# Attention in 64-by-192 halves with one division per token tile, weights bit-converted on VectorE in SBUF and checked late, a rational activation by completed squares, and a new order

## The chip, the cores and the metric

The kernel runs on one core of a Trainium2 chip. The core has a matrix engine (TensorE, PE in the profile), VectorE (DVE), ScalarE (ACT), GpSimd (POOL) and an engine that only issues transfers here (SyncE, SP). The metric is the device time of one launch in microseconds.

## What is computed

Three stages in a row on 1536 tokens (2 batches of 768): an attention of 8 heads of 64, in which a query sees the 96 keys up to itself and the first 8 of the sequence; a feed-forward layer ("MoE 1", 512 to 2048 to 512) whose activation is a ratio of two polynomials; and a second one ("MoE 2", 512 to 1024 to 512) with a softmax gate and a layer norm between its products. The weights arrive as 64-bit floats.

```
keep = is_global | is_local                      # 8 first keys, 96 keys up to the query
a = softmax(where(keep, q @ k.T / 8 - slope[h] * dist, -1e9))
x = (a @ v) with the heads side by side          # 1536 x 512

h = x @ w_in                                     # 512 -> 2048
P = a[0] + a[1]*h + a[2]*h*h + a[3]*h*h*h
Q = 1 + |b[0]|*|h| + |b[1]|*h*h
x = (P / (Q + 1e-6)) @ w_out                     # 2048 -> 512

h = x @ w2_in                                    # 512 -> 1024
solu = h * softmax(h)
ln = (solu - mean) / sqrt(var + 1e-6) * g_ln
out = ln @ w2_out                                # 1024 -> 512
```

## The kernel before

The 1536 tokens are 12 tiles of 128, in 4 blocks of three tiles (384 tokens). The attention works in **units**: one tile and one pair of heads, 48 in all. 8 of them (first tile of a sequence) see 128 keys, the other 40 see 256, of which the mask leaves what counts. One unit goes through all engines: SP loads queries and keys and then values; PE makes the scores (line 459, two matmuls; in blocks 0 and 3 each head's 64 rows of the array work beside the other's into two banks, in blocks 1 and 2 both heads go one after the other through all 128 rows into one bank); DVE adds the bias and finds the maximum (464); ACT takes the exponential with its row sum (471); DVE inverts the sum (476, 477); POOL or, for the 19 units of `NDVE`, DVE multiplies by it (482); PE transposes (502, four of 128 by 128); ACT copies to SBUF (514); PE multiplies with the values (509); ACT and DVE split the result into a rounded high part and a rest (516 and the helper in line 99). `x` in such pairs is the left side of MoE 1.

**MoE 1** runs in 64 **steps**, one for each group of 128 hidden units and block: 12 matmuls of 128x384 for `h` (634, 636 and 640: high times high, high times low, low times high), an epilogue on ACT, DVE and POOL (660 to 677 and the helper), and, three steps later (`LAG`), 9 matmuls of 128x512 that add into the three `y` banks (725, 726, 731). Block 0 comes first with 8 of its 16 groups, then blocks 1 to 3, then block 0 again with the rest (`SEGS`). The attention units of the next block are laid between the steps of the current one (`UW`). The epilogue before is, in order: c = a3*h + a2 (ACT 660), times h (DVE 662), |b0*h| (ACT 663), c = (c + a1)*h (DVE 664), h squared in PSUM (ACT 666), q (DVE 667), 1/Q as exp(-ln) (ACT 669, 670) with a Newton step (DVE 671, 673), times P (DVE 675), rounded copy (ACT 677), rest (POOL, line 99).

**Weights**: 48 tiles of 128x512 64-bit floats, 512 KB each. Of each an ACT multiply (565) and integer operations on DVE make a 32-bit float, for 22 tiles three (569, 570, 574), for the 26 of `ZS` a POOL multiply (582) and two on DVE (586, 574); the half-made words lie in a PSUM bank of the attention's. Then ACT rounds (604) and POOL, or DVE for the 6 of `WDVE`, takes the rest (99).

**MoE 2** goes tile by tile: 24 matmuls (810 to 812), maximum and softmax and norm on DVE and ACT (832 to 854, 857, 859), transposes (872), split (880, 99), 24 matmuls (894 to 896, the last tile in quarters), output.

**What sets the order**: every operation is recorded with an estimated duration and what it reads and writes; a planner (`Plan`) works out due times, shifted by kind with the table `LEADS`, and emits each engine's instructions in one fixed order. PSUM has 8 banks: two for `h`, two `s` (scores, weight conversion), one `p` (transposes, values), three for `y`. In gaps that the planner expects on PE early on, it emits dummy matmuls of the identity (line 337, 51 of them in before). A flag (lines 1187 to 1194), worked out from the mask's sizes, says whether a general slow path must follow.

## Time and profile before

| | us |
|---|---|
| three runs | 557.36, 557.90, 558.82 |
| median | 557.9 |
| span of the profiled execution | 556.3 |
| PE busy | 531.8 (96%) |
| DVE busy | 446.0 (80%) |
| ACT busy | 393.0 (71%) |
| POOL busy | 182.5 (33%) |

Beside its span the profiled execution has no other time in the page; the median of the runs is 1.6 us above the span. Busy shares are means over stages with different limits: the start (attention alone, up to 43.66 us), MoE 1 with attention and weight conversion beside it (up to about 408 us), and MoE 2. PE's busy time includes a matmul's way through the array, so gaps shorter than that don't show in it; what PE has to do is better read from the distance of starts in the timeline.

### The profile page before, as it was taken

Reading aid. Unit: us, or ns where it says so; the run is one execution under the profiler, and the core shown is the slowest. Engines: PE = TensorE matmul, PEld = TensorE weight load, DVE = VectorE, ACT = ScalarE, POOL = GpSimd, SP = SyncE. Lnnn points to the kernel's source line nnn. Section 1 sums busy time; section 2 is a strip of 40 time slices with the busy share of each in tenths; the row PEclk is TensorE's granted clock in tenths of the full one; section 3 lists DMA queues with packets and bytes.
Section 4 is the critical chain, followed back from the end, with each engine's and each line's share of the span. In section 5 each row is a group of like instructions: output and inputs, shape, how many; then the busy total and the mean of one; then the engine's idle time right before and its main releaser. Section 6 shows DMA issues by size and latency. Waiting matters only on the chain.

```text
span 556.3 us, 8937 instructions
## 1 busy us (share of the span) xinstructions
PE 531.8 (96%) x2910; PEld 437.0 (79%) x2910; DVE 446.0 (80%) x1104; ACT 393.0 (71%) x911; POOL 182.5 (33%) x212
## 2 busy tenths in 40 slices
...
PEclk9999999999999999999999999999999999999999
...
GB/s 252 130 201 341 195 219 86 185 135 153 104 182 154 151 96 98 73 48 48 1 38 114 133 77 75 77 180 87 57 20 38 39 38 58 20 19 20 19 39 43
DMA packets 28278, 56.24 MB, mean 101 GB/s; under 512 B 3520, under 2 KB 11968, under 8 KB 28224
## 3 DMA queue, kind: packets, MB, share of 16 engines
...
q8 instruction: 25, 0.41, 0.3%
q14 instruction: 29, 0.24, 0.1%
q10 hardware_dynamic: 144, 0.00, 0.0%
HBM read 47.72 MB, written 7.86 MB: 100 GB/s over the span
## 4 chain that ended last, share of the span: by engine, by line
PE 55%; DVE 29%; ACT 10%; issue 4%; DMA 1%; POOL 0%; SPq 0%; ACTq 0%; DVEq 0%; POOLq 0%
PE pb L894 4%; PE pb L896 4%; PE pb L895 4%; PE pb L634 4%; PE pb L810 4%; PE pb L812 4%; PE pb L811 4%; PE pb L640 4%; PE pb L731 3%; PE pb L636 3%; PE pb L725 3%; DVE t L667 3%; PE pb L459 3%; DVE wst L574 3%; PE pb L726 3%
## 5 line engine op out<-in xcount | busy, mean ns | idle before, releaser
L99 POOL TENSOR_TENSOR g<-t,g 128x384 fp32r<-128x384 f32 x64 | 69.2, 1082 | 103.9 <-ACT g L677 91.7
L634 PE MATMUL pb<-x,w 128*128 128x384 f32 x256 | 89.3, 349 | 1.8 <-DVE t L667 1.8
L636 PE MATMUL pb<-x,w 128*128 128x384 f32 x256 | 86.1, 336 | 0.0
L725 PE MATMUL pb<-w,g 128*128 128x512 f32 x192 | 77.5, 404 | 4.2 <-ACT g L677 4.2
L726 PE MATMUL pb<-w,g 128*128 128x512 f32 x192 | 75.6, 394 | 0.5 <-POOL w L99 0.5
L99 POOL TENSOR_TENSOR w<-wst,w 128x512 fp32r<-128x512 f32 x42 | 57.2, 1364 | 42.7 <-ACT w L604 38.8
L640 PE MATMUL pb<-x,w 128*128 128x384 f32 x256 | 58.0, 347 | 0.1
L731 PE MATMUL pb<-w,g 128*128 128x512 f32 x192 | 57.7, 409 | 0.2 <-POOL g L99 0.2
L634 PEld LDWEIGHTS pb<-x,w 128*128 128x128 f32 x256 | 48.1, 188 | 8.6 <-DVE t L667 4.4
L471 ACT ACTIVATE e<-e,st 128x256 f32<-128x256 f32 (+1 forms) x96 | 46.3, 486 | 6.4 <-DVE st L464 6.4
L640 PEld LDWEIGHTS pb<-x,w 128*128 128x128 f32 x256 | 44.5, 188 | 7.1 <-issue 3.1
L636 PEld LDWEIGHTS pb<-x,w 128*128 128x128 f32 x256 | 48.1, 188 | 1.5
L725 PEld LDWEIGHTS pb<-w,g 128*128 128x128 f32 x192 | 36.0, 187 | 14.4 <-ACT g L677 7.3
L660 ACT ACTIVATE t<-pb,coef 128x384 f32<-128x384 f32 x64 | 42.7, 668 | 6.1 <-PE pb L640 6.1
L482 POOL TENSOR_SCALAR e<-e,st 128x256 f32<-128x256 f32 (+1 forms) x58 | 28.0, 495 | 54.4 <-DVE st L477 48.4
L669 ACT ACTIVATE t<-t,coef 128x384 f32<-128x384 f32 x64 | 39.6, 618 | 6.8 <-DVE t L667 6.6
L662 DVE TENSOR_TENSOR t<-t,pb 128x384 f32<-128x384 f32 x64 | 35.2, 549 | 11.1 <-ACT t L663 6.5
L677 ACT CAST g<-t 128x384 fp32r<-128x384 f32 x64 | 32.8, 512 | 16.0 <-DVE t L675 15.3
L880 ACT CAST lh<-pb 128x512 fp32r<-128x512 f32 x24 | 13.9, 592 | 42.5 <-PE pb L872 42.5
L459 PE MATMUL pb<-qk 64*128 64x256 f32 (+3 forms) x192 | 41.3, 393 | 2.7 <-DVE st L464 1.0
L667 DVE SCALAR_TENSOR_TENSOR t<-pb,coef,t 128x384 f32<-128x384 f32 x64 | 39.2, 613 | 5.2 <-ACT pb L666 4.8
L671 DVE SCALAR_TENSOR_TENSOR t<-t,t 128x384 f32<-128x384 f32 x64 | 40.6, 634 | 1.3 <-ACT t L670 1.3
...
## 6 DMA issues: line engine op xcount, KB each, us to landing
...
```

The lines of the kernel that those rows point to most:

```text
L99: eng.tensor_tensor(out=out, in0=a, in1=hi.bitcast(F32), op=ALU.subtract)
L459: pe.matmul(out=score(h), lhsT=a[r, h * 128:(h + 1) * 128], rhs=a[r, 256:256 + w], start=True, stop=True)
L471: act.activation(out=e[:, h, 0:w], in_=e[:, h, 0:w], func=AF.Exp, scale=-1.0, bias=st[:, h:h + 1], accum_out=st[:, 2 + 2 * h:3 + 2 * h])
L634: pe.matmul(out=pb[:, g.h.slot, 0:n], lhsT=wt[wh.slot][:, cs[p]], rhs=xt[x[p][0].slot][:, 0:n], start=(p == 0), stop=False)
L636: pe.matmul(out=pb[:, g.h.slot, 0:n], lhsT=wt[wl.slot][:, cs[p]], rhs=xt[x[p][0].slot][:, 0:n], start=False, stop=False)
L640: pe.matmul(out=pb[:, g.h.slot, 0:n], lhsT=wt[wh.slot][:, cs[p]], rhs=xt[x[p][1].slot][:, 0:n], start=False, stop=(p == 3))
L660: op("ACT", 0.2 + 0.46 * k, lambda: act.activation(out=T(g.c), in_=h(), func=AF.Identity, scale=coef[:, 3:4], bias=coef[:, 2:3]), r=[g.h], ...
L667: op("DVE", 0.2 + 0.41 * k, lambda: stt_(out=T(g.a), in0=h(), scalar=coef[:, 5:6], in1=T(g.b), op0=ALU.mult, op1=ALU.add), r=[g.h, g.b], n ...
L671: op("DVE", 0.15 + 0.41 * k, lambda: stt_(out=T(g.a), in0=T(g.a), scalar=1.0 + 1e-6, in1=T(g.b), op0=ALU.add, op1=ALU.mult), r=[g.b], w=[g ...
L725: pe.matmul(out=pb[:, y[i].slot, :], lhsT=gt[g.gh.slot][:, c], rhs=wt[wh.slot], start=g.first, stop=False)
L726: pe.matmul(out=pb[:, y[i].slot, :], lhsT=gt[g.gh.slot][:, c], rhs=wt[wl.slot], start=False, stop=False)
L731: pe.matmul(out=pb[:, y[i].slot, :], lhsT=gt[g.gl.slot][:, c], rhs=wt[wh.slot], start=False, stop=g.last)
```

## The change

Attention units of the 40 kind now take 64 queries by 192 keys each: four score matmuls of 64 rows by 64 columns of the array with 192 moving columns (line 571), three transposes (601) instead of four, one exponential of 192 (585). The values' product is turned round (614): the transposed weights are stationary and the values move, in three pairs of column halves, and the four units of a tile add into one bank. Nothing is divided in a unit; per tile one inversion (631, 632), one multiplication of 128x512 out of PSUM on DVE (637), four transposes (641) and one split (649, 149) stand in the place of four of each. ACT or, for 10 units of `TRX`, DVE copies the transposed weights (619).

Weight conversion is three DVE integer operations (705, 709, 713) in an SBUF buffer `cvt`; the ACT and POOL multiplies are gone. The new operations hold for exponents in a usual range only. The rounding goes to ACT (28), POOL (13) or DVE (7) by `WHX`; the rest to DVE 17 times. Whether the exponents lie in that range is found out during MoE 2: all 48 weight tiles are loaded again (25 MB) and one DVE operation each (763, 765) collects the bits; a small tree, one matmul and the flag stand at the end of the program, and the engines load the flag there.

The polynomials are written with completed squares: c is one ACT square of a scaled and shifted h (826), and the multiplication by h (662 before) and the square in PSUM (666 before) are gone. q is, for 32 steps of `SQX`, another ACT square (832) and for 32 a DVE operation (836). The exponential's result lies in SBUF for 16 steps and in PSUM banks `p` or `s` for 48 (`EPX`). The rounded copy goes to ACT (33), POOL (16) or DVE (15) by `GHX`. A sign that the squares leave over is multiplied in when `y` leaves PSUM. Some 20 small DVE and 4 small ACT operations that work out the new coefficients are added at the start. `SPILL`'s reload goes from ACT and POOL to DVE. All tables (`LEADS`, `UW`, `WS`, `M2`, `BACK`) are new; dummy matmuls before MoE 1 are 18 instead of 51. The queries, keys and values of a unit are 448 KB instead of 384.

```diff
-UW = {1: (0, 7), 2: (8, 15), 3: (25, 14)}
+UW = {1: (1, 4), 2: (8, 15), 3: (25, 9)}
...
+WS = (1, 24)
+
+M2 = (29, 35)
+
+WSB, TB, GB, QB, VB, EB, YB, PB = 4, 8, 4, 3, 4, 3, 4, 1
+
+WLEAD = 33.8
...
+BACK = (('y1', 'p'), ('y0', 'y2'), 's')
+
+QK = 'hhhhhhhhhhhhmmtmmmmmmmmmmtttmmmmhmmmmtmmmmmmmmtt'
+BANKS_OF = {"h": "hh", "t": "ss", "m": "hs"}
...
+SQX = 'AAADAAAAAAAAAAAAAAAAAAAADDDDDDDDDDDDAAAADDAAAAADDDDDDDDDDDDDDDDD'
+EPX = 'ttpspptsppsssssspppptpppttssttttptppppttppssppppstpspppspssstsst'
+TRX = 'DAAADADADAADDDAAAAAAAAAADAAAAAAAAAAAAADDAAAAAAAA'
+GHX = 'AAAAAAAAAADPAAAAPDDADDADDDAAPADPPAPDDAAADAAAPPPDDPPPADPPPAAAAAAP'
+WHX = 'PAPDAAAAPPPAAAPAAAAAAAAAAAPPDAADDAAAAPPDDPAPAADP'
+WDVE = (1, 4, 6, 11, 14, 18, 22, 25, 26, 27, 29, 30, 33, 35, 38, 41, 43)
...
-FILL = (30.0, 0.45, 0.25)
+FILL = (0.7, 0.45, 0.4, 0.25)
...
+        a, b = (256, 384) if u.first else (384, 896)
+        uop("SP", 2.4, lambda: sync.dma_start(out=qkt[u.qk.slot][:, 0:a], in_=qkv[u.t, u.p, :, 0:a]), occ=0.4,
+            new=[u.qk], move=0.6, tag="ld")
+        uop("SP", 2.4, lambda: sync.dma_start(out=vt[u.v.slot][:, 0:b - a], in_=qkv[u.t, u.p, :, a:b]), occ=0.4,
+            new=[u.v], move=0.2 if u.first else 0.8, tag="ld")
...
-                r = slice(h * 64, (h + 1) * 64) if two else slice(0, 128)
-                pe.matmul(out=score(h), lhsT=a[r, h * 128:(h + 1) * 128], rhs=a[r, 256:256 + w], start=True, stop=True)
+                r = slice(h * 64, (h + 1) * 64)
+                if u.first:
+                    pe.matmul(out=score(h), lhsT=a[r, 0:128], rhs=a[r, 128:256], start=True, stop=True)
+                else:
+                    for c in (0, 64):
+                        pe.matmul(out=pb[c:c + 64, u.s[h].slot, 0:w], lhsT=a[r, c:c + 64], rhs=a[r, 128 + c:128 + c + w], start=True, stop=True)
...
-        def recip():
-            st = stt[u.st.slot]
-            dve.tensor_scalar(out=st[:, 3:6:2], in0=st[:, 2:5:2], scalar1=1e-9, scalar2=None, op0=ALU.add)
-            dve.reciprocal(out=st[:, 6:8], in_=st[:, 3:6:2])
...
+            for c in range(0, 2 * u.w, 128):
+                pe.transpose(out=pb[:, u.pp.slot, c:c + 128], in_=et[u.e.slot][:, c:c + 128], identity=ident)
...
+            for c, n_, d_, v_ in ((0, 64, d, 0), (128, 128, d, 128), (256, 64, d + 64, 384)):
+                for g in (0, 1):
+                    x = c + g * 64
+                    pe.matmul(out=pb[g * 64:(g + 1) * 64, tl.acc.slot, d_:d_ + n_], lhsT=pt[:, x:x + 64],
+                              rhs=v[:, v_ + g * n_:v_ + (g + 1) * n_], start=(u.p == 0 and c == 0), stop=(c == 256), skip_group_check=True)
...
         def norm():
-            e, st = et[u.e.slot], stt[u.st.slot]
-            for h in range(2):
-                (dve if ndve else pool).tensor_scalar(out=e[:, h, 0:w], in0=e[:, h, 0:w], scalar1=st[:, 6 + h:7 + h],
-                                                      scalar2=0.0, op0=ALU.mult, op1=ALU.add)
...
-            uop("DVE", 0.24 + 0.15 * n, norm, r=[u.st], w=[u.e], lock=True, occ=0.12 + 0.15 * n, tag="norm")
-        else:
-            uop("POOL", 0.63 + 0.2 * n, norm, r=[u.st], w=[u.e], lock=True, occ=0.6 + 0.2 * n, tag="norm")
...
+            x, r = bass.broadcast_tensor_aps(pb[:, tl.acc.slot, :].rearrange("p (h d) -> p h d", h=8),
+                                             stt[tl.st.slot][:, 2, :].rearrange("p (h o) -> p h o", o=1))
+            dve.tensor_tensor(out=xqt[tl.xq.slot].rearrange("p (h d) -> p h d", h=8), in0=x, in1=r, op=ALU.mult)
...
-                for k in range(n):
-                    c = (h * n + k) * 128
-                    pe.transpose(out=pb[:, u.pp.slot, c:c + 128], in_=et[u.e.slot][:, h, k * 128:(k + 1) * 128], identity=ident)
...
-                    v0 = k * 128 + h * 64
-                    pe.matmul(out=pb[h * 64:(h + 1) * 64, u.xp.slot, 0:128], lhsT=vt[u.v.slot][:, v0:v0 + 64],
-                              rhs=ptt[:, c:c + 128], start=(k == 0), stop=(k == n - 1))
...
+        uop("PE", 0.74, tr, r=[tl.xq], new=[tl.xp], occ=0.44, tag="xT")
+        uop("ACT", 0.59, lambda: act.copy(xt[a.slot][:, :, cs], xT()), r=[tl.xp], w=[a], tag="xh")
+        uop("DVE", 0.68, lambda: minus(nc, dve, xt[b.slot][:, :, cs], xT(), xt[a.slot][:, :, cs]), r=[tl.xp, a], w=[b], tag="xl")
...
-                u.w = 128 if u.first else 256
+                u.w = 128 if u.first else 192
...
+        if eng == "A":
+            op("ACT", 0.13 + 0.00098 * n, lambda: act.copy(out(), src()), **k)
+        elif eng == "D":
+            op("DVE", 0.18 + 0.00052 * n, lambda: dve.tensor_copy(out(), src()), lock=True, **k)
+        else:
+            op("POOL", 0.1 + 0.00104 * n, lambda: pool.tensor_copy(out(), src()), lock=True, **k)
...
-            act.mul(a.bitcast(F32), w1.bitcast(F32), 2.0 ** -112)
-
-        def bits():
-            w0, w1, a = words()
-            dve.scalar_tensor_tensor(out=a, in0=a, scalar=3, in1=w1, op0=ALU.logical_shift_left, op1=ALU.bitwise_xor)
-            dve.scalar_tensor_tensor(out=a, in0=w1, scalar=0x7FFFFFFF, in1=a, op0=ALU.bitwise_and, op1=ALU.bitwise_xor)
...
-            pool.tensor_scalar(out=w1, in0=w1, scalar1=2.0 ** -100, scalar2=2.0 ** -100, op0=ALU.mult, op1=ALU.mult)
...
+            dve.tensor_scalar(out=o, in0=w1, scalar1=3, scalar2=0x3FFFFFFF, op0=ALU.logical_shift_left, op1=ALU.bitwise_and)
...
+            dve.scalar_tensor_tensor(out=o, in0=w1, scalar=-0x40000000, in1=o, op0=ALU.bitwise_and, op1=ALU.bitwise_or)
...
+            dve.scalar_tensor_tensor(out=wst[st.slot][:, 0:512], in0=w0, scalar=29, in1=o, op0=ALU.logical_shift_right, op1=ALU.bitwise_or)
...
+                dve.scalar_tensor_tensor(out=a, in0=w1, scalar=0x40000000, in1=a, op0=ALU.bitwise_xor, op1=ALU.bitwise_and)
+
+        op("SP", 2.0, lambda: sync.dma_start(out=words(), in_=src.bitcast(I32)), occ=0.42, new=[st], move=2.0, after=gl[-4:] + joins[-1:], tag="ckl")
+        op("DVE", 0.7, seen, r=[st], **{"new" if first else "w": [vacc]}, tag="ck")
...
-        op("ACT", 0.2 + 0.46 * k, lambda: act.activation(out=T(g.c), in_=h(), func=AF.Identity, scale=coef[:, 3:4], bias=coef[:, 2:3]),
...
-        op("DVE", 0.14 + 0.41 * k, lambda: dve.tensor_tensor(out=T(g.c), in0=T(g.c), in1=h(), op=ALU.mult), r=[g.h], w=[g.c], tag="ch")
-        op("ACT", 0.15 + 0.42 * k, lambda: act.activation(out=T(g.b), in_=h(), func=AF.Abs, scale=coef[:, 4:5]), r=[g.h], new=[g.b], tag="abs")
-        op("DVE", 0.2 + 0.41 * k, lambda: stt_(out=T(g.c), in0=T(g.c), scalar=coef[:, 1:2], in1=h(), op0=ALU.add, op1=ALU.mult),
...
+        op("ACT", 0.2 + 0.46 * k, lambda: act.activation(out=T(g.c), in_=h(), func=AF.Square, scale=poly[:, 0:1], bias=poly[:, 1:2]),
...
+        op("ACT", 0.15 + 0.42 * k, lambda: act.activation(out=T(g.b), in_=h(), func=AF.Abs, scale=poly[:, 4:5]), r=[g.h, vpoly], new=[g.b], tag="abs")
+        op("DVE", 0.2 + 0.41 * k, lambda: stt_(out=T(g.c), in0=T(g.c), scalar=poly[:, 2:3], in1=h(), op0=ALU.add, op1=ALU.mult),
...
-        op("ACT", 0.1 + 0.38 * k, lambda: act.activation(out=h(), in_=h(), func=AF.Square), w=[g.h], tag="sq")
-        op("DVE", 0.2 + 0.41 * k, lambda: stt_(out=T(g.a), in0=h(), scalar=coef[:, 5:6], in1=T(g.b), op0=ALU.mult, op1=ALU.add),
...
...
+        if k2 == "A":
+            op("ACT", 0.17 + 0.42 * k, lambda: act.activation(out=T(g.a), in_=T(g.b), func=AF.Square, bias=poly[:, 7:8]),
...
+            add, one = poly[:, 8:9], poly[:, 8:9]
+        else:
+            op("DVE", 0.2 + 0.43 * k, lambda: stt_(out=T(g.a), in0=T(g.b), scalar=poly[:, 5:6], in1=T(g.b), op0=ALU.add, op1=ALU.mult),
...
+            add, one = coef[:, 6:7], 1.0 + 1e-6
+        new = {"w": [g.b]} if lk else {"new": [g.e]}
+        op("ACT", 0.22 + 0.4 * k, lambda: act.activation(out=T(g.e), in_=T(g.a), func=AF.Ln, bias=add), r=[g.a], **new, tag="ln")
+        op("ACT", 0.15 + 0.38 * k, lambda: act.activation(out=T(g.e), in_=T(g.e), func=AF.Exp, scale=-1.0), w=[g.e], tag="ex")
+        op("DVE", 0.15 + 0.41 * k, lambda: stt_(out=T(g.a), in0=T(g.a), scalar=one, in1=T(g.e), op0=ALU.add, op1=ALU.mult),
...
+            for key in (wseq + w2seq)[6 * k - 6:6 * k]:
+                w_check(key)
...
+            op("DVE", 2.2, w_verdict, w=[vacc, vbad], tag="flag")
+            op("POOL", 0.3, lambda: pool.memset(ones, 1.0), r=[vacc], w=[vones], tag="ck")
+            op("PE", 0.3, lambda: pe.matmul(out=pb[:, bank.slot, 0:1], lhsT=ones, rhs=bad, start=True, stop=True), r=[vbad, vones], new=[bank], occ=0.1, tag="ck")
+            op("DVE", 0.2, lambda: flag.weights(pb[:, bank.slot, 0:1]), r=[bank], w=[vflag], tag="flag")
```

PE just ahead of the first matmul of MoE 1, before (`pb` is a PSUM bank, `e` the exponentials, `qk` and `v` the loaded parts, `pt` the transposed weights).

```order
L459 MATMUL pb<-qk_205 128x256 x2
L509 MATMUL pb<-pt,v_208 64x128 x4
L502 MATMUL pb<-ident,e_214 128x128 x4
L459 MATMUL pb<-qk_206 128x256 x2
L509 MATMUL pb<-pt,v_209 64x128 x4
L459 MATMUL pb<-qk_204 128x256 x2
L509 MATMUL pb<-pt,v_210 64x128 x4
L502 MATMUL pb<-ident,e_211 128x128 x4
L634 MATMUL pb<-x_173,w_92 128x384
```

The same place after; `xq` is a whole tile's result after the division.

```order
L571 MATMUL pb<-qk_181 64x192 x4
L614 MATMUL pb<-v_186,pt_190 64x64 x2
L614 MATMUL pb<-v_186,pt_190 64x128 x2
L614 MATMUL pb<-v_186,pt_190 64x64 x2
L601 MATMUL pb<-ident,e_187 128x128 x3
L641 MATMUL pb<-ident,xq 128x128 x4
L614 MATMUL pb<-v_183,pt_190 64x64 x2
L614 MATMUL pb<-v_183,pt_190 64x128 x2
L614 MATMUL pb<-v_183,pt_190 64x64 x2
L601 MATMUL pb<-ident,e_188 128x128 x3
L797 MATMUL pb<-x_161,w_87 128x384
```

The pairs of 128x256 scores became four of 64x192 in a row, the values' four became three pairs, and a tile ends with four transposes of its own.

DVE in the middle of MoE 1, before: `t` are epilogue buffers, 128x384 rows are the epilogue, 128x256 an attention unit.

```order
L667 SCALAR_TENSOR_TENSOR t_163<-pb,coef,t_162 128x384
L671 SCALAR_TENSOR_TENSOR t_160<-t_160,t_168 128x384
L673 SCALAR_TENSOR_TENSOR t_168<-t_160,t_168 128x384
L675 SCALAR_TENSOR_TENSOR t_167<-t_167,coef,t_168 128x384
L464 ISA e_213,st_218<-pb,bt_200 128x256
L464 ISA st_218 128x1
L464 ISA e_213,st_218<-pb,bt_201 128x256
L464 ISA st_218 128x1
L662 TENSOR_TENSOR t_166<-t_166,pb 128x384
L664 SCALAR_TENSOR_TENSOR t_166<-t_166,coef,pb 128x384
L476 TENSOR_SCALAR st_218<-st_218 128x2
```

DVE at such a place after; `poly` holds the new coefficients, `xq` the divided tile, `g` the rounded copy.

```order
L637 TENSOR_TENSOR xq<-pb,st_191 128x512
L829 SCALAR_TENSOR_TENSOR t<-t,poly,pb 128x384
L844 SCALAR_TENSOR_TENSOR t<-t 128x384
L846 SCALAR_TENSOR_TENSOR t<-t,poly 128x384
L920 TENSOR_SCALAR y_165<-pb,poly 128x512
L671 CAST g_159<-t 128x384
L842 SCALAR_TENSOR_TENSOR t<-t,pb 128x384
L844 SCALAR_TENSOR_TENSOR pb<-t,pb 128x384
L846 SCALAR_TENSOR_TENSOR t<-t,poly,pb 128x384
L149 TENSOR_TENSOR x_164<-pb,x_163 128x4x128
L836 SCALAR_TENSOR_TENSOR t<-t,poly 128x384
```

The row that multiplied c by h is gone, a step has four or five epilogue rows instead of five with 662, and one multiplication of 128x512 stands for a tile's divisions; a rounded copy (671) has come to DVE.

DVE in MoE 2, before: one tile from its maximum's sign to its norm.

```order
L833 TENSOR_SCALAR st_2941<-st_2941 128x1
L99 TENSOR_TENSOR ll_2945<-pb,lh_2943 128x512
L99 TENSOR_TENSOR yl_2939<-pb,yh_2937 128x512
L836 TENSOR_SCALAR st_2941<-st_2941 128x1
L837 RECIPROCAL st_2941<-st_2941 128x1
L838 SCALAR_TENSOR_TENSOR wst_156,st_2941<-pb,st_2941,wst_156 128x1024
L839 TENSOR_SCALAR st_2941<-st_2941 128x1
L843 TENSOR_SCALAR st_2941<-st_2941 128x1
```

After, with the checks of reloaded weights (765) in between.

```order
L1000 TENSOR_SCALAR st_2599<-st_2599 128x1
L149 TENSOR_TENSOR yl_2597<-pb,yh_2595 128x512
L149 TENSOR_TENSOR ll_2605<-pb,lh_2603 128x512
L765 SCALAR_TENSOR_TENSOR cv<-t,cv 128x512
L1003 TENSOR_SCALAR st_2599<-st_2599 128x1
L1004 RECIPROCAL st_2599<-st_2599 128x1
L1005 SCALAR_TENSOR_TENSOR wst_153,st_2599<-pb,st_2599,wst_153 128x1024
L1006 TENSOR_SCALAR st_2599<-st_2599 128x1
L149 TENSOR_TENSOR ll_2605<-pb,lh_2603 128x512
L765 SCALAR_TENSOR_TENSOR cv<-t,cv 128x512 x2
```

The checks stand singly and in twos between the steps of a tile's softmax and norm, so that what follows on DVE waits for them and for their loads.

## Rows read from the trace of the kernel before

**Rows 1.** The page: busy time of the engines; by slices TensorE's clock and the transfers.

```profile
PE 531.8 (96%) x2910; PEld 437.0 (79%) x2910; DVE 446.0 (80%) x1104; ACT 393.0 (71%) x911; POOL 182.5 (33%) x212
...
PEclk9999999999999999999999999999999999999999
...
GB/s 252 130 201 341 195 219 86 185 135 153 104 182 154 151 96 98 73 48 48 1 38 114 133 77 75 77 180 87 57 20 38 39 38 58 20 19 20 19 39 43
```

**Rows 2.** Busy time in the start, MoE 1, a stretch of it, and MoE 2.

```profile
core 0: us, PE busy (x) PEld busy (x) DVE busy (x) ACT busy (x) POOL busy (x), PEclk, DMA share, GB/s
0.00:43.66 43.66, 39.12 (x291) 29.37 (x291) 34.50 (x154) 30.35 (x102) 11.03 (x25) 1.00 0.62 200
43.66:390.40 346.74, 335.26 (x1846) 276.93 (x1844) 320.51 (x739) 296.59 (x677) 162.71 (x179) 1.00 0.38 121
200.00:300.00 100.00, 99.94 (x573) 80.95 (x571) 83.48 (x214) 80.22 (x191) 28.55 (x32) 1.00 0.17 52
410.00:547.00 137.00, 135.29 (x665) 112.64 (x666) 74.53 (x180) 54.84 (x111) 1.99 (x2) 1.00 0.10 33
```

**Rows 3.** The same view: four steps with attention, four without, and the steps behind.

```profile
116.50:141.30 24.80, 23.43 (x123) 19.00 (x122) 24.32 (x52) 20.62 (x48) 15.46 (x18) 1.00 0.56 166
282.80:299.60 16.80, 16.80 (x86) 15.18 (x85) 13.35 (x23) 13.46 (x29) 6.19 (x8) 1.00 0.10 33
299.60:390.40 90.80, 86.76 (x425) 75.55 (x425) 88.29 (x157) 77.65 (x152) 49.13 (x47) 1.00 0.34 114
```

**Rows 4.** PE's waits: line, whom for, us in all, times, longest.

```profile
PE pb L725 <- ACT g L677: 4.2, 7, 1.0
PE pb L634 <- DVE t L667: 1.8, 3, 0.8
```

**Rows 5.** PE's timeline (start, us): a unit of block 0, two banks; records in twos.

```profile
28.08 0.66 PE L509 MATMUL pb<-pt,v 128*64 128x128 f32 x8
28.67 0.66 PE L502 MATMUL pb<-ident,e 128*128 128x128 f32 x4
29.25 0.70 PE L459 MATMUL pb<-qk 64*128 64x256 f32 x4
29.88 0.33 PE L502 MATMUL pb<-ident,e 128*128 128x128 f32 x1
```

**Rows 6.** PE's timeline: units with one bank, and MoE 1's first matmul.

```profile
41.59 1.13 PE L459 MATMUL pb<-qk 128*128 128x256 f32 x4
42.66 0.66 PE L509 MATMUL pb<-pt,v 128*64 128x128 f32 x8
43.24 0.66 PE L502 MATMUL pb<-ident,e 128*128 128x128 f32 x4
43.66 0.42 PE L634 MATMUL pb<-x,w 128*128 128x384 f32 x1
```

**Rows 7.** Groups of the epilogue and attention: busy us, mean ns | idle before, releaser.

```profile
L662 DVE TENSOR_TENSOR t<-t,pb 128x384 f32<-128x384 f32 x64 | 35.2, 549 | 11.1 <-ACT t L663 6.5 <-ACT t L660 4.4
L667 DVE SCALAR_TENSOR_TENSOR t<-pb,coef,t 128x384 f32<-128x384 f32 x64 | 39.2, 613 | 5.2 <-ACT pb L666 4.8 <-POOL w L99 0.2
L677 ACT CAST g<-t 128x384 fp32r<-128x384 f32 x64 | 32.8, 512 | 16.0 <-DVE t L675 15.3
L464 DVE CUSTOM_DVE_ANT_0 e<-pb,bt 128x256 f32<-128x256 f32 x80 | 30.5, 418 | 1.4 <-PE pb L459 1.0
L482 DVE TENSOR_SCALAR e<-e,st 128x256 f32<-128x256 f32 x36 | 12.1, 379 | 0.4
L477 DVE RECIPROCAL st<-st 128x2 f32<-128x2 f32 x48 | 8.0, 167 | 1.6
L99 DVE TENSOR_TENSOR x<-pb,x 128x128 fp32r<-128x128 f32 x48 | 13.6, 284 | 2.3 <-ACT x L516 2.0
```

**Rows 8.** Groups of the weight conversion, and a one-source DVE operation of MoE 2.

```profile
L574 DVE SCALAR_TENSOR_TENSOR wst<-wst,pb 128x512 int32<-128x512 int32 x48 | 32.7, 680 | 0.3
L586 DVE SCALAR_TENSOR_TENSOR pb<-pb,wst 128x512 int32<-128x512 int32 x26 | 18.0, 692 | 0.3 <-POOL wst L582 0.3
L570 DVE SCALAR_TENSOR_TENSOR pb<-wst,pb 128x512 int32<-128x512 int32 x22 | 15.3, 696 | 0.7
L569 DVE SCALAR_TENSOR_TENSOR pb<-pb,wst 128x512 int32<-128x512 int32 x22 | 15.2, 692 | 0.9 <-ACT pb L565 0.8
L854 DVE TENSOR_SCALAR wst<-wst,st 128x1024 f32<-128x1024 f32 x12 | 9.8, 813 | 0.4
```

**Rows 9.** DVE in MoE 2 waiting for a tile's second half.

```profile
L832 DVE TENSOR_REDUCE st<-pb 128x1 f32<-128x1024 f32 x12 | 14.7, 1224 | 28.2 <-PE pb L812 28.2
```

544 lines of the change are left out of this document (326 added, 218 removed).

## The prediction

> **What bounds the kernel now.** I read the page's busy times first: PE is busy 96% of the span, DVE 80%, ACT 71%, POOL 33%, and TensorE's clock is granted in full in every slice [rows 1]. So PE sets the time, if at all, through how much it has to do and how often it is made to wait. Busy time hides short waits, because a matmul counts as busy for its whole way through the array; so I counted work by starts. Four steps of MoE 1 without attention, 84 matmuls, take 16.8 us at most when nothing disturbs them [rows 3], that is 0.200 us each (16.7 with two stray records less), and all 64 steps 16 x 16.7 = 267 us. A unit of attention with two banks has starts 0.59 us apart for values, 0.58 (0.42 where PE goes straight on to a matmul) for transposes, 0.63 for scores [rows 5]; with one bank the scores take 1.07 [rows 6]. With 0.45 for the transposes that is 1.67 and 2.10 us, 20 units each, and about 1 us for each of the 8 small ones: 83 us of attention.
>
> MoE 1's first matmul starts at 43.66 [rows 6]. Ahead of it PE works on 4 small units, 8 whole ones and the scores of four more, about 22 us; the other 22 are idle or dummy. From 43.66 to 390.4 lie 347 us [rows 2]; the work in it is 61 us of attention (83 - 22) and MoE 1 less its last three y's (267 - 6), so 322. **Some 25 us are waiting.** Where? Two rows show the pattern: with DVE at 13.35 of 16.8 us (79%) PE loses nothing, with DVE at 88.3 of 90.8 (97%) 425 matmuls, 85 us of work, take 90.8; with 24.32 of 24.8 (98%) four steps with two units, 16.7 + 4.2, take 24.8 [rows 3]. Also from 200 to 300 us DVE is at 83% and PE is full [rows 2]. PE's listed waits name what DVE feeds: y waits for the rounded copy on ACT, which itself sat idle 15.3 us for DVE's last epilogue operation, and h for the bank that DVE's q frees [rows 4, 7]. So MoE 1 is bound by PE and DVE together, and the start by DVE with its 34.5 us in 43.7 [rows 2].
>
> **Start.** Taken from DVE before MoE 1's first matmul: ten units' divisions (20 x 0.379 = 7.6), 13 pairs of small inverse operations (13 x 2 x 0.167 = 4.3), scores of 192 in place of 256 columns (24 x 0.418 against 20 x 0.335, that is -3.3, the 0.335 an estimate between 0.314, in proportion, and the row itself), splits (13 x 0.284 against 3 at 0.68, -1.7): -17 [rows 7]. Added: six copies out of PSUM (6 x 0.5, by columns from 0.68 for 512 [rows 8]), three divisions of a tile (3 x 0.68), a further 512-wide split (0.68), new coefficients (some 20 tiny operations at 0.167, 3.4 [rows 7]); the weights there are four with three operations as before: +9. Net -8, of which I take 6.7, since the chain of units has its own length: first matmul at 37. Bounds: 33 and 42 (nothing, but for half a unit). What hides a change here is PE's idleness, 22 us before, 17 then. TensorE's clock was granted in full with 51 dummy matmuls there [rows 1]; with 18 it may drop to 1.2 GHz between, and 20 us of work at half rate, half of it covered by idle time, would add up to 5.
>
> **Attention on PE.** Scores: the 0.63 holds two heads beside each other with 256 columns; with 192 it is 0.47, plus one more pair started, 0.52 if the two query halves also run beside each other. Values: three pairs with 256 columns in all as before, plus a pair's start, 0.64. Transposes: three in place of four, which took 0.42 to 0.58, 0.35. Transposes of the tile: 0.42 in four units, 0.11. Sum 1.62, against 1.67 and 2.10: 20 x 0.05 + 20 x 0.48 = 10.6 less about 1.5 for the small units, which gain a tile's transposes: 74 us in all, 20 ahead of MoE 1 and 54 behind. **-7 in MoE 1.** The scores have no row with four quadrants; the bounds are 0.47 and 0.94 (two pairs one after the other), I take the near end because head pairs by rows and value pairs by columns both run beside each other [rows 5].
>
> **Waits in MoE 1.** DVE there: 320.5 us [rows 2]. Off: the multiplication by h, 64 x 0.549 = 35.2; 32 q's, 32 x 0.613 = 19.6; attention, 32 units' share of inversions, divisions, splits and narrower maxima less the tile's own and 4 copies, about 14 [rows 7]. On: weights, 48 x (0.69 + 0.69 + 0.42) and 17 rests at 0.69 and 7 rounded copies at 0.4, against 81 + 4 before: +16, 14 of it here [rows 8]; 15 rounded copies 5.7; four reloads 2.4. The first of the three conversions has one source; I price it by half the 0.81 us of the one-source row with 1024 columns, and its upper bound is 0.69, +13 in all [rows 8]. Sum 320.5 - 68.8 + 22.1 = 274 us on DVE beside 315 on PE (54 + 261): 87%, against 99% before. By stages, counting the instructions of both orders, it is still 104 to 111% of PE in steps 1 to 12 and 76 to 96% after. In the first 12 steps DVE stays the bound and costs about 5 us, in the rest I take 3% of 260, the loss between the stretch at 83% and that at 97%: 7. **12 us of waits in place of 25, so -13**, bounds 5 and 24. ACT loses c's neighbour h squared and the conversion's multiply and gains 32 q's: far from full. The Trainium skill ("ScalarE: Activation LUTs", Rules for kernel authors) says simple arithmetic belongs on VectorE and not on ScalarE, which speaks against the 32 squares on ACT. By the rows the two are alike for this size, 613 ns on DVE and 512 for a plain ACT pass [rows 7]; leaving them on DVE would put DVE at 93%.
>
> **MoE 2.** 48 operations of 0.65 us, 31 us, come to DVE, which is busy 74.5 of 137 us [rows 2]: 77% then. Of each tile's slack DVE spends 28.2 / 11 = 2.6 us waiting for PE at one place alone [rows 9], and four to six checks (at most 4 us) come to a tile. What stands behind a check is the next step of a softmax, and PE's transposes behind that; it has another tile's products to go on with. The reloads, 25 MB in eight tiles' time of 11.4 us, are 275 GB/s beside 33 [rows 2], near the 341 of the busiest slice [rows 1]; a check whose load is late holds DVE's queue and the softmax behind it. I take +1, bounds 0 and 12. **End**: flag loads and one matmul after the last output's work, +0.4.
>
> **Sum.** -6.7 - 7 - 13 + 1 + 0.4 = -25.3; span 556.3 - 25.3 = 531, and 1.6 us more for the median, as before: **532.6**.
>
> **Rivals.** *PE's waits vanish*: if 87% on DVE is as harmless as 83% is in rows 2 and the start reaches 33, another 11 us go, 520. For it: every row below 85% shows none. Against: the first 12 steps.
>
> *Banks take the place of DVE.* 48 steps now put their exponential in banks that also serve scores, transposes and a tile's sum, and 28 units' scores take one of the two h banks. h matmuls then wait until DVE's maximum has read the bank, which the list already shows in small [rows 4]. At 0.4 to 0.7 us for half of the 32 later units and 48 steps that is 16 to 28 us, and the waits stay where they were: 541 to 552, centre 545. A conversion's first operation at 0.69, or a clock that falls at the start, ends in the same place. For it: four engines meet in one or two banks. Against: the weight conversion left the same banks.
>
> *Slower: the four score matmuls go one after another.* In one bank a score matmul of 256 columns takes 1.07 / 2 = 0.53 us [rows 6], of 192 then 0.40, and four 1.60 in place of 0.52: 40 x 1.08 = 43 us on PE, of which the start hides about 10: 532.6 + 33 = 566. It decides from about 0.64 us a unit (25.3 / 40) above my price on. Rows show pairs by rows and pairs by columns [rows 5], never both. The Trainium skill ("TensorEngine Tiling (Array Packing)", Key Properties) states that a change of tiling mode drains TensorE, and a unit now changes it four times. The trace agrees: four transposes take 0.58 us where a 64-row matmul follows and 0.42 where a 128-row one does [rows 5, 6]. The units of before with two banks pay that already; by the difference, 0.16 us, the 20 others would now pay 3 us in all.
>
> *It doesn't do what it says*: all gains off the path, within 0.3% of now, about what a measurement of this kernel can tell from no change.
>
> **Chances.** Forecast (525 to 540) 0.45; waits vanish (515 to 525) 0.17; banks or DVE stay (540 to 554) 0.26; no change 0.03; slower 0.09. Faster by over 0.3% is the first three less the edge of the third, 0.87; the same 0.04. The range takes the second case's lower end and most of the third: 516 to 549.
>
> **What would show it.** First h matmul near 37; four 64x192 records within 0.55 us; DVE 79 to 90% between steps 12 and 64 and PE's waits there under 8 us; DVE 105 us in MoE 2 with the last matmul some 137 us after MoE 1. Wrong if score rows stand over 1 us apart, if the waits name h after the maxima, or if MoE 2 is longer by over 6 us.

## The result and the profile after

The changed kernel takes **552.6 us** (551.6 to 555.4 in five runs) against 558.8 for the kernel before, timed beside it: a ratio of 0.9896, interval 0.9869 to 0.9922. It is faster by 1.0%, 6 us, where 25 were forecast, and outside the range of 516 to 549. The profiled execution spans 549.8 us.

The page of the changed kernel, busy times and TensorE's granted clock by slices, for [rows 1]:

```profile
PE 525.0 (95%) x3224; PEld 434.3 (79%) x3224; DVE 469.3 (85%) x1046; ACT 319.9 (58%) x733; POOL 138.3 (25%) x144
...
PEclk9899898999999999999999999999999999999998
```

PE has less to do (531.8 before), ACT and POOL far less, and **DVE more**: 469 against 446 us. 32 us of that are the checks in MoE 2, but in MoE 1 it lost a multiplication of 35 us in all and half of the q's. And the clock, granted in full throughout before, is not in four slices.

Busy time of the engines by stretches (the same columns as in [rows 2]): the start up to the first matmul of MoE 1, MoE 1 up to its last hidden matmul, and the stretch that was compared before:

```profile
core 0: us, PE busy (x) PEld busy (x) DVE busy (x) ACT busy (x) POOL busy (x), PEclk, DMA share, GB/s
37.92:377.70 339.78, 327.85 (x2099) 273.37 (x2098) 308.57 (x620) 232.48 (x521) 114.14 (x111) 0.99 0.40 127
0.00:37.92 37.92, 32.20 (x307) 23.01 (x307) 28.04 (x119) 22.82 (x80) 7.11 (x16) 0.95 0.72 223
200.00:300.00 100.00, 99.92 (x657) 84.13 (x654) 89.06 (x183) 68.16 (x153) 27.75 (x27) 1.00 0.28 88
```

The first matmul of MoE 1 starts at 37.92 (43.66 before; 37 was forecast). In MoE 1 DVE is busy for 308.6 us; the prediction's sum was 274. Counted as the prediction counted, PE's work in these 339.8 us is 54 of attention and 267 less 63 y matmuls that come later at 0.23, 14.5: 306.5. **33 us are waiting**; the prediction said 12 in place of some 25. (Before, 36 y matmuls come later than 390.4, not the 27 that the prediction took, so by the same count its waits were 27.)

Where DVE's 34.6 us more come from stands in its groups (busy us, mean ns of one, idle before). These are the conversion's three operations, two of the epilogue, and one of the epilogue in its two forms, for [rows 7, 8]:

```profile
L713 DVE SCALAR_TENSOR_TENSOR wst<-wst,cv 128x512 int32<-128x512 int32 x48 | 41.6, 868 | 1.0
L709 DVE SCALAR_TENSOR_TENSOR cv<-wst,cv 128x512 int32<-128x512 int32 x48 | 39.2, 817 | 1.5
L829 DVE SCALAR_TENSOR_TENSOR t<-t,poly,pb 128x384 f32<-128x384 f32 x64 | 38.7, 606 | 3.8 <-ACT t L828 3.4 <-ACT t L826 0.2
...
L836 DVE SCALAR_TENSOR_TENSOR t<-t,poly 128x384 f32<-128x384 f32 x32 | 27.1, 846 | 2.3 <-ACT t L828 2.2
...
L844 DVE SCALAR_TENSOR_TENSOR pb<-t,pb 128x384 f32<-128x384 f32 x48 | 26.8, 558 | 1.0
...
L705 DVE TENSOR_SCALAR cv<-wst 128x512 int32<-128x512 int32 x48 | 24.9, 519 | 0.1
...
L844 DVE SCALAR_TENSOR_TENSOR t<-t 128x384 f32<-128x384 f32 x16 | 11.6, 726 | 0.2
```

The same operation, line 844, takes 558 ns on average where one operand lies in PSUM (`pb`) and 726 where all lie in SBUF. What an average hides, the spread of one line shows (duration of one, min/median/max):

```profile
L713 DVE SCALAR_TENSOR_TENSOR wst<-wst,cv x48: 639/690/1664, 14.1 to 396.8; 128x512 int32<-128x512 int32 x48
...
L829 DVE SCALAR_TENSOR_TENSOR t<-t,poly,pb x64: 598/606/615, 42.3 to 382.2; 128x384 f32<-128x384 f32 x64
```

35 of the 48 joins (713) take 0.64 to 0.70 us, the other 13 up to 1.66; the operation with an operand in PSUM (829) varies by 17 ns in 64. The checks of MoE 2 (765), which have the conversion's shape and lie in SBUF alone, vary by 18 ns in 47 (676 to 694): GpSimd is busy for only 4 of the 135 us around them. Above their medians (690, 693, 420 for the conversion, 618 for q) the four lines alone lose 48 x (0.178 + 0.124 + 0.099) + 32 x 0.228 = 27 us; with the other SBUF-only lines, each against its own median, the sum is near 37 in the whole span, against 9 in the kernel before.

One place shows what the long ones wait for. DVE's, GpSimd's and PE's timelines around 85 us (start, duration, us):

```profile
84.51 1.45 DVE L705 TENSOR_SCALAR cv<-wst 128x512 int32<-128x512 int32 x1
85.99 1.36 DVE L709 SCALAR_TENSOR_TENSOR cv<-wst,cv 128x512 int32<-128x512 int32 x1
87.28 0.68 DVE L637 TENSOR_TENSOR xq<-pb,st 128x512 f32<-128x512 f32 x1
```

```profile
84.41 1.27 POOL L149 TENSOR_TENSOR w<-wst,w 128x512 fp32r<-128x512 f32 x1
85.64 1.17 POOL L149 TENSOR_TENSOR g<-t,g 128x384 fp32r<-128x384 f32 x1
```

```profile
84.86 0.94 PE L389 MATMUL pb<-ident 128*128 128x128 f32 x6
88.02 0.65 PE L641 MATMUL pb<-ident,xq 128*128 128x128 f32 x4 [2.22 <-DVE xq L637]
88.43 0.52 PE L797 MATMUL pb<-x,w 128*128 128x384 f32 x1
```

The conversion's first operation starts 0.1 us after the start of a GpSimd subtraction and ends 0.3 us after its end; the second meets the next subtraction and does the same. 0.42 + 0.69 us of work have become 2.8 us, the tile's division (637), due next on DVE, starts 1.7 us later than it could, and PE stands for 2.22 us, the longest wait in its list. Then its clock falls: the matmul behind takes 0.52 in place of 0.42 and the ones after it start 0.32 us apart in place of 0.17.

This is the rule and not one place. 62 VectorE operations in the trace take over 0.1 us more than their line's median, and each of them meets a GpSimd operation that began first (25 before); none has an operand in PSUM. Of the lines 705, 709, 713 and 836, every operation but one that began inside a GpSimd subtraction with over 0.1 us to go is among them. The eight long ones of line 705 end 0.28 us after the GpSimd operation, the thirteen of 713 0.49 to 0.55, the twelve of 836 0.41 to 0.42: their undisturbed time less 0.14 to 0.2 us, as if their work began only when GpSimd's was done. The planner of both kernels knows of it: operations marked `lock` in the code, the conversion and the q's among them, are planned never to run beside a GpSimd operation so marked. But it fixes the order ahead and not the times, and so they meet.

### The profile page after: what moved, and what is told of

It reads as the page before. It is cut to its first block, busy times and chain, and to the rows that moved or that the text cites. A ratio compares the mean times of both kernels' runs of the same rounds, so it can differ in the third digit from the quotient of the medians.

```text
span 549.8 us, 9337 instructions
## 1 busy us (share of the span) xinstructions
PE 525.0 (95%) x3224; PEld 434.3 (79%) x3224; DVE 469.3 (85%) x1046; ACT 319.9 (58%) x733; POOL 138.3 (25%) x144
## 4 chain that ended last, share of the span: by engine, by line
PE 56%; DVE 30%; ACT 9%; issue 3%; DMA 0%; ACTq 0%; DVEq 0%
PE pb L1062 4%; PE pb L1064 4%; DVE t L842 4%; PE pb L1063 4%; PE pb L979 4%; PE pb L977 4%; PE pb L978 4%; PE pb L797 4%; PE pb L614 4%; PE pb L799 4%; PE pb L803 3%; DVE t L846 3%; DVE t L836 3%; DVE pb L844 3%; DVE cv L709 3%
## 5 line engine op out<-in xcount | busy, mean ns | idle before, releaser
L149 POOL TENSOR_TENSOR w<-wst,w 128x512 fp32r<-128x512 f32 x31 | 41.7, 1347 | 79.0 <-ACT w L669 42.7
L826 ACT ACTIVATE t<-pb,poly 128x384 f32<-128x384 f32 x64 | 42.8, 668 | 25.1 <-PE pb L803 16.2
L797 PEld LDWEIGHTS pb<-x,w 128*128 128x128 f32 x256 | 48.8, 191 | 8.4 <-DVE t L829 5.7
L799 PEld LDWEIGHTS pb<-x,w 128*128 128x128 f32 x256 | 48.9, 191 | 1.5
L585 ACT ACTIVATE e<-e,st 128x192 f32<-128x192 f32 (+1 forms) x96 | 41.9, 439 | 13.9 <-DVE st L577 13.7
L803 PEld LDWEIGHTS pb<-x,w 128*128 128x128 f32 x256 | 45.2, 190 | 5.4 <-issue 1.7
L890 PEld LDWEIGHTS pb<-w,g 128*128 128x128 f32 x192 | 36.0, 188 | 10.6 <-DVE y L920 2.7
L713 DVE SCALAR_TENSOR_TENSOR wst<-wst,cv 128x512 int32<-128x512 int32 x48 | 41.6, 868 | 1.0
L829 DVE SCALAR_TENSOR_TENSOR t<-t,poly,pb 128x384 f32<-128x384 f32 x64 | 38.7, 606 | 3.8 <-ACT t L828 3.4
L828 ACT ACTIVATE t<-pb,poly 128x384 f32<-128x384 f32 x64 | 36.9, 577 | 7.8 <-DVE t L844 4.4
L891 PEld LDWEIGHTS pb<-w,g 128*128 128x128 f32 x192 | 36.1, 188 | 5.8
L709 DVE SCALAR_TENSOR_TENSOR cv<-wst,cv 128x512 int32<-128x512 int32 x48 | 39.2, 817 | 1.5
L1062 PE MATMUL pb<-w,lh 128*128 128x512 f32 (+1 forms) x104 | 40.1, 386 | 0.0
L1064 PE MATMUL pb<-w,ll 128*128 128x512 f32 (+1 forms) x104 | 39.1, 376 | 0.0
L896 PEld LDWEIGHTS pb<-w,g 128*128 128x128 f32 x192 | 34.0, 188 | 6.0 <-issue 2.2
```

What stands on the lines that cost most here:

```text
L149: eng.tensor_tensor(out=out, in0=a, in1=hi.bitcast(F32), op=ALU.subtract)
L585: act.activation(out=x, in_=x, func=AF.Exp, scale=-1.0, bias=st[:, 0, c:c + 1], accum_out=st[:, 1, c:c + 1])
L709: dve.scalar_tensor_tensor(out=o, in0=w1, scalar=-0x40000000, in1=o, op0=ALU.bitwise_and, op1=ALU.bitwise_or)
L797: pe.matmul(out=pb[:, g.h.slot, 0:n], lhsT=wt[wh.slot][:, cs[p]], rhs=xt[x[0].slot][:, p, 0:n], start=(p == 0), stop=False)
L799: pe.matmul(out=pb[:, g.h.slot, 0:n], lhsT=wt[wl.slot][:, cs[p]], rhs=xt[x[0].slot][:, p, 0:n], start=False, stop=False)
L803: pe.matmul(out=pb[:, g.h.slot, 0:n], lhsT=wt[wh.slot][:, cs[p]], rhs=xt[x[1].slot][:, p, 0:n], start=False, stop=(p == 3))
```

## The experiments

All times are medians; ratios are to the kernel before, run beside each. The changed kernel itself has 0.9896. Steps of MoE 1 are counted from the last hidden matmul of the first to that of the last.

**GpSimd's subtractions shortened, in the changed kernel and in the one before.** The cut, in the first:

```diff
-lambda: minus(nc, pool, gt[g.gl.slot][:, 0:n], T(g.c), gt[g.gh.slot][:, 0:n])
+lambda: minus(nc, pool, gt[g.gl.slot][:, 0:8], T(g.c)[:, 0:8], gt[g.gh.slot][:, 0:8])
...
-minus(nc, pool, wt[lo.slot], src(), wt[hi.slot])
+minus(nc, pool, wt[lo.slot][:, 0:8], src()[:, 0:8], wt[hi.slot][:, 0:8])
```

The order of the instructions stays; the matmuls that read the subtractions' results read the rounded part instead, so the low-order terms are left out.

> The changed kernel with GpSimd's two kinds of subtraction (the rest of the activation, 64 of 1.11 us; the rest of the weights, 31 of 1.35 us) cut to 8 columns, in the same planned order; the matmuls read the rounded part in place of the rest, so the result lacks the low-order terms. In the changed kernel VectorE's operations with every operand in SBUF are stretched now and then (conversion 817 and 868 ns on average against a median of 690, q 846 against 616), 35 us in all; operations with an operand in PSUM are not (606, at most 615). Theory 'shared port': a VectorE operation on SBUF alone stands until a running GpSimd operation ends, and this keeps VectorE the bound of MoE 1. It expects the means to fall to the medians, VectorE's busy time from 469 to about 435 us and the time from 552.6 to 533 to 541 us. Theory 'banks' (PE and the epilogue wait for PSUM banks that scores, exponentials and sums share): VectorE's means may fall, the time stays within 550 to 553 us.

539.0 us, 0.9628 (0.9581 to 0.9676): **13.6 us less** than the changed kernel. The same groups of DVE, and the stretch of MoE 1 without attention:

```profile
L709 DVE SCALAR_TENSOR_TENSOR cv<-wst,cv 128x512 int32<-128x512 int32 x48 | 34.2, 712 | 1.5
L713 DVE SCALAR_TENSOR_TENSOR wst<-wst,cv 128x512 int32<-128x512 int32 x48 | 33.1, 689 | 1.2 <-DVE cv L709 0.5
...
L836 DVE SCALAR_TENSOR_TENSOR t<-t,poly 128x384 f32<-128x384 f32 x32 | 20.0, 625 | 3.4 <-ACT t L828 3.3
```

```profile
265.00:366.00 101.00, 100.95 (x507) 91.00 (x507) 86.47 (x158) 64.41 (x120) 19.85 (x48) 1.00 0.29 91
```

The means fall to the medians, DVE's total to 436 us, and PE is full (100.95 of 101.0) where the changed kernel has

```profile
271.00:377.00 106.00, 101.94 (x500) 89.22 (x499) 99.40 (x157) 62.28 (x117) 47.02 (x48) 1.00 0.27 85
```

In this run PE no longer needs the subtractions' results either. But no wait on them stood in PE's list of the changed kernel, so it isn't their results that PE waited for. 'Shared port' holds in size and sign; 'banks' doesn't explain this loss.

> A control: the kernel before with the same two kinds of GpSimd subtraction cut to 8 columns in its own order (low-order terms left out as in the short run of the changed kernel). Before, the conversion and the multiplication by h had an operand in PSUM, and the planner kept the few operations of SBUF alone apart. Theory 'the change brought the stretch': at most 5 us less than before, 553 to 558. Rival 'before is as much held by the port as after, so that the changed kernel only inherits it': 13 us less, 543 to 547.

553.5 us, 0.9882 (0.9850 to 0.9914): 5.8 us less than the kernel before beside it, between the two expectations. Before, too, had some of it: its Newton operations on SBUF alone (671, 673) fall from 634 and 601 ns on average to 562 and 567. So the change raised what these subtractions cost from 6 to 14 us, it didn't invent it. The trace of before had it in plain sight, in the spread of two lines of like work:

```profile
L671 DVE SCALAR_TENSOR_TENSOR t<-t,t x64: 536/551/1419, 52.6 to 397.1; 128x384 f32<-128x384 f32 x64
```

```profile
L574 DVE SCALAR_TENSOR_TENSOR wst<-wst,pb x48: 666/680/695, 15.4 to 410.9; 128x512 int32<-128x512 int32 x48
```

**GpSimd's activation subtraction done twice**, the opposite dose:

```diff
-lambda: minus(nc, pool, gt[g.gl.slot][:, 0:n], T(g.c), gt[g.gh.slot][:, 0:n]),
+lambda: [minus(nc, pool, gt[g.gl.slot][:, 0:n], T(g.c), gt[g.gh.slot][:, 0:n]) for _ in (0, 1)],
```

> The changed kernel with GpSimd's subtraction of the activation's rest done twice over in the same place (64 more operations of 1.11 us, 71 us on an engine that is busy for 138 of 550), in the same planned order. Theory 'shared port': VectorE's operations on SBUF alone meet GpSimd more often, their stretch grows from 35 to some 50 or 60 us, those with an operand in PSUM stay as they are, and the time grows by 6 to 14 us: 559 to 567. Rival 'GpSimd is off the path': 552 to 555, VectorE's busy time unchanged.

571.6 us, 1.0231 (1.0197 to 1.0265): 19 us more, beyond the expected 14. DVE's groups:

```profile
L709 DVE SCALAR_TENSOR_TENSOR cv<-wst,cv 128x512 int32<-128x512 int32 x48 | 45.6, 950 | 1.5
L713 DVE SCALAR_TENSOR_TENSOR wst<-wst,cv 128x512 int32<-128x512 int32 x48 | 43.6, 908 | 1.0
L829 DVE SCALAR_TENSOR_TENSOR t<-t,poly,pb 128x384 f32<-128x384 f32 x64 | 38.8, 607 | 5.4 <-ACT t L828 5.2 <-ACT t L826 0.2
```

DVE's busy time rises by 24 us with not one instruction more; 829, on PSUM, stays at 607. PE's list now has h waiting 11.1 us for 829, which stands behind the long ones on DVE's queue. (The result of the subtraction is also 1.1 us later; PE's waits for it are 0.4 us in all.)

**The conversion's buffer back in PSUM**, in one of the two banks of scores and transposes:

```diff
-            return w[:, :, 0], w[:, :, 1], cvt
+            return w[:, :, 0], w[:, :, 1], pbi[:, cv.slot, :]
...
-        cv = Val("cv")
+        cv = Val("s", "conv")
```

The edit also takes the `lock` from the three operations, and the planner makes a new order.

> The changed kernel with the half-made words of the weight conversion in a PSUM bank, as before the change, in place of the SBUF buffer; one of the two banks of scores and transposes is taken by each of the 48 conversions for its time, and the planner makes a new order for it. Theory 'shared port': the three conversion operations have an operand in PSUM and keep to their medians (0.42, 0.69, 0.69 us), which takes 19 of the 35 us of stretch away: 5 to 10 us less, 543 to 548. Theory 'banks': the two banks are the scarce thing and are now taken for another 48 x 2 us: 5 to 15 us more, 557 to 567.

572.5 us, 1.0237 (1.0191 to 1.0283): 20 us more. The conversion keeps to 0.69 us (means 687, 695, 681), as 'shared port' says, though the first operation, 0.42 us in SBUF, takes 0.69 on PSUM; and yet the kernel is slower, by more than 'banks' said. PE's list:

```profile
PE pb L797 <- DVE t L829: 6.3, 8, 3.0
PE pb L890 <- ACT g L669: 4.6, 1, 4.6
...
PE pb L568 <- DVE wst L713: 1.5, 1, 1.5
```

The last line is a bank that the conversion holds: scores and transposes wait for its last operation for 3.5 us in all. The rest is not shown to be banks. MoE 1 is 22.6 us longer, and 19.7 of them lie in one place, from the first hidden matmul of step 13 to that of step 17 (45.2 us in place of 25.5), where PE waits for one engine after the other, 4.6 us of it for a copy on ACT, and the granted clock falls to 0.50. So the run shows that PSUM keeps GpSimd away from the conversion; that banks are the dearer price stays open, since the new order was not told apart from them.

**The exponential of all steps in SBUF** (`EPX` all `t`):

```diff
-EPX = 'ttpspptsppsssssspppptpppttssttttptppppttppssppppstpspppspssstsst'
+EPX = 't' * 64
```

> The changed kernel with the exponential of all 64 steps in SBUF (16 there before, 48 in the banks of scores and sums). Theory 'shared port': 96 Newton operations of 0.55 to 0.61 us have every operand in SBUF then and stretch by 0.1 to 0.2 on average as the 16 steps' did (726 against 558): VectorE 10 to 20 us more, 557 to 567. Theory 'banks': 48 holdings of the p and s banks go, scores and transposes get them earlier: 540 to 549.

590.7 us, 1.0561 (1.0538 to 1.0585). The sign is that of 'shared port' (844 at 680 ns for all 64 now, 558 on PSUM), the size is not: DVE's total rises by 20 us only, the time by 38. The epilogue buffers are taken for longer then, 144 more operations are held apart from GpSimd's by the planner, and its new order has 241 dummy matmuls, in gaps that it foresaw, where the changed kernel has 43. The run tells that the 48 steps in PSUM are worth having in these orders, not why in full.

**Block 1's units over six steps in place of four:**

```diff
-UW = {1: (1, 4), 2: (8, 15), 3: (25, 9)}
+UW = {1: (1, 6), 2: (8, 15), 3: (25, 9)}
```

> The changed kernel with the 12 attention units of block 1 laid over six steps of MoE 1 in place of four (one table entry). In the changed kernel steps 1 to 8 take 54.7 us for some 39 us of matmuls, the largest loss of any stretch. Theory 'crowding' (weights, units and epilogue of these steps together overload VectorE): 4 to 8 us less, 545 to 549. Theory 'shared port': the same operations stand beside GpSimd wherever they are; within 2 us of 552.6.

550.1 us, 0.9844 (0.9797 to 0.9890): 2.5 us less, at the edge of what the intervals tell apart, where 'crowding' expected 4 to 8 and 'shared port' up to 2; steps 4 to 8 take 41.2 us in place of 44.8. **With dummies in smaller gaps besides:**

```diff
-FILL = (0.7, 0.45, 0.4, 0.25)
+FILL = (0.25, 0.45, 0.4, 0.25)
```

> The run with block 1's units spread over six steps, and dummy matmuls already in planned gaps of 0.25 us instead of 0.7: 53 in place of 43. In the changed kernel TensorE's granted clock falls to 0.6 in three stretches of 4 us in the first 92 us (about 1.6 us each). Theory 'clock' (this is a good part of the missing gain): no stretch below 0.9 and 545 to 548 us against 550. Rival: the dips follow stalls that dummies of planned gaps don't fill: 549 to 552 with the dips still there.

548.7 us, 0.9808 (0.9792 to 0.9825). Three stretches of the changed kernel, with the granted clock third from the end of each row:

```profile
16.00:20.00 4.00, 3.70 (x21) 2.64 (x22) 1.73 (x4) 1.35 (x3) 1.31 (x1) 0.61 0.63 197
64.00:68.00 4.00, 4.00 (x28) 3.38 (x25) 2.87 (x6) 1.07 (x3) 1.02 (x1) 0.59 0.59 154
88.00:92.00 4.00, 3.98 (x16) 3.99 (x17) 3.40 (x7) 2.07 (x4) 0.00 (x0) 0.57 0.35 141
```

and with more dummies:

```profile
16.00:20.00 4.00, 3.44 (x29) 2.42 (x30) 2.56 (x6) 1.41 (x4) 1.76 (x2) 1.00 0.72 212
60.00:68.00 8.00, 6.84 (x81) 5.12 (x73) 7.35 (x23) 6.13 (x17) 2.31 (x2) 1.00 0.73 230
84.00:92.00 8.00, 7.58 (x53) 7.08 (x54) 7.22 (x12) 5.53 (x11) 3.24 (x3) 1.00 0.63 181
```

A stretch at 0.6 is one at 1.2 GHz for most of 4 us; two of them came behind waits of PE that end at 63.5 and 88.0 in its timeline. The low clock is gone, as 'clock' said, but the dummies cured only the first stretch. The spread units alone had already ended the other two:

```profile
16.00:20.00 4.00, 3.27 (x20) 2.69 (x24) 1.69 (x3) 0.54 (x2) 1.52 (x1) 0.73 0.75 212
64.00:68.00 4.00, 3.75 (x38) 3.06 (x36) 3.71 (x9) 2.50 (x8) 0.71 (x1) 1.00 0.77 246
88.00:92.00 4.00, 4.00 (x22) 3.62 (x21) 3.71 (x7) 3.24 (x7) 0.71 (x1) 1.00 0.67 245
```

Against them 1.4 us go, at the edge of what the intervals tell apart, and in the traces they go in the start: MoE 1's first matmul comes at 37.7 with the dummies and at 39.1 without, and from there to the last hidden matmul both take 337 us.

**All three at once**, the shortened subtractions with these two edits:

```diff
+UW = {1: (1, 6), 2: (8, 15), 3: (25, 9)}
+FILL = (0.25, 0.45, 0.4, 0.25)
```

> The changed kernel with all three of the suspected costs lessened at once: GpSimd's subtractions cut to 8 columns (low-order terms left out), block 1's units over six steps, more dummy matmuls. If the three add up, 13.6 + 2.5 + 1.4 us go from 552.6: 534 to 537, and little is left to the forecast of 532.6. If they are the same loss seen three ways: 538 to 541.

540.1 us, 0.9656 (0.9623 to 0.9689), no less than the short subtractions alone: the spread and the dummies give nothing more that can be told once GpSimd is out of the way. In the traces the first matmul of MoE 1 comes 3.4 us earlier, at 37.3 (the short run's granted clock was 0.63 and 0.50 between 16 and 24 us), but MoE 1 is 2.2 us longer. That the spread lessens a loss which the long DVE operations cause is a reading of this; no run shows it alone. Runs of this kernel lie between 538.3, with a mean granted clock of 0.999, and 541.1, with 0.989.

**The rechecks of MoE 2 left out:**

```diff
-        if wide and 1 <= k <= 8:
+        if False and wide and 1 <= k <= 8:
```

> The changed kernel without the second load of the weights, the 48 bit operations in MoE 2 and the verdict (the range of the exponents isn't looked at). MoE 2's tiles follow each other in the changed kernel as fast as before (first score matmul of the first and of the last tile 126.6 us apart, 126.9 before), so the reading is that the checks are hidden: 550.5 to 553 us. The rival, that they hold VectorE's queue in MoE 2 and cost the 6 us by which MoE 2 with its end seems longer from MoE 1's last hidden matmul on: 545 to 548 us.

552.0 us, 0.9864 (0.9816 to 0.9913): no difference to the changed kernel can be told. The 32 us of DVE and 25 MB of loads are hidden.

**q of all steps on ScalarE** (with the spread units), then every rounded copy too:

```diff
-SQX = 'AAADAAAAAAAAAAAAAAAAAAAADDDDDDDDDDDDAAAADDAAAAADDDDDDDDDDDDDDDDD'
+SQX = 'A' * 64
```

> The run with block 1's units spread over six steps, and q of all 64 steps as a square on ScalarE; the planner makes its order anew. 32 VectorE operations of SBUF alone, 27 us with their stretch, go; ScalarE, 59% busy, gets 32 of about 0.62. Theory 'shared port': the bound of MoE 1 is lightened by a fifth of what the short GpSimd run showed to matter twice over, 541 to 546 us against 550. Theory 'banks': the exponentials wait for their banks as before, 549 to 552. A third, that the planner's new order is worse than the tuned one: above 553.

546.8 us, 0.9778 (0.9761 to 0.9794): 3.3 us less than the spread units alone, a little short of the 4 to 9 expected. Steps 40 to 64, where 19 of the 32 q's stood on DVE, take 101 us in place of 107; steps 20 to 24 take 25.6 in place of 23.9 in the new order.

```diff
-GHX = 'AAAAAAAAAADPAAAAPDDADDADDDAAPADPPAPDDAAADAAAPPPDDPPPADPPPAAAAAAP'
-WHX = 'PAPDAAAAPPPAAAPAAAAAAAAAAAPPDAADDAAAAPPDDPAPAADP'
+GHX = 'A' * 64
+WHX = 'A' * 48
```

> As the run before, and every rounded copy too (16 of the activation and 13 of the weights from GpSimd, 15 and 7 from VectorE) on ScalarE. GpSimd keeps only the subtractions. Theory 'shared port': fewer GpSimd operations meet fewer VectorE ones; VectorE's conversion means fall below 800 ns; 538 to 544 us. The rival is that ScalarE, then some 70% busy, delivers the rounded copies late and PE's y matmuls wait for it: 548 to 556, with y waiting for the copy in PE's list.

550.4 us, 0.9839 (0.9821 to 0.9857): 3.7 us worse again. DVE is down to 437 us, but steps 16 to 24 take 60.2 us in place of 50.9, and PE's list has scores waiting 2.5 us for DVE's maximum and values 2.6 us for the copy on ACT. y doesn't wait for the rounded copy, as the rival said; it is attention that is late in this order.

And the edits that helped, together:

```diff
+UW = {1: (1, 6), 2: (8, 15), 3: (25, 9)}
+SQX = 'A' * 64
+FILL = (0.25, 0.45, 0.4, 0.25)
```

> The whole computation: q of all steps on ScalarE, block 1's units over six steps, more dummy matmuls. If the dummies' gain adds to that of q: 544.5 to 546 us. If the new order has no low clock to cure: 546.5 to 547.5.

546.7 us, 0.9778 (0.9749 to 0.9806): the whole computation with q on ScalarE, spread units and more dummies is faster than both kernels and no better than q and spread alone. Its six runs go from 545.1 to 549.4 us with the mean granted clock from 0.999 down to 0.986; a hundredth of the clock is worth some 3 us.

## Why the prediction was wrong, step by step

**Start: right.** 37.92 for 37, from 43.66. The unknown that was priced at nothing, the clock with fewer dummies, cost something: the granted clock of the start is 0.95, and falls to 0.61 between 16 and 20 us. How much, varies: with the same planned order another execution (the short subtractions) had a granted clock of 0.50 to 0.63 from 16 to 28 us and its first matmul at 40.8. With five more dummies the clock stayed at 1.00 there and the first matmul came at 37.7.

**Attention on PE: right.** PE's timeline of the changed kernel, two units:

```profile
67.56 0.80 PE L601 MATMUL pb<-ident,e 128*128 128x128 f32 x3
68.29 0.56 PE L571 MATMUL pb<-qk 64*64 64x192 f32 x8
68.78 0.96 PE L803 MATMUL pb<-x,w 128*128 128x384 f32 x4
69.66 0.67 PE L614 MATMUL pb<-v,pt 128*64 128x64 f32 x12
70.26 0.56 PE L571 MATMUL pb<-qk 64*64 64x192 f32 x8
```

The scores take 0.49 us from their start to the next (0.52 said), the values 0.60 (0.64). The three transposes, for which 0.35 was said, take 0.24 where a 128-row matmul follows and 0.48 where a 64-row one does (medians of the whole trace; the 0.73 above still stands in the stretch at 1.2 GHz). All four quadrants work beside each other, in 0.49 us for four matmuls of which one bank's single one took 0.53 with 256 columns [rows 6]; the slower rival falls, and with it its price of 1.08 us a unit.

**Waits in MoE 1: wrong, and this is the miss.** The prediction put DVE at 274 us, and waits at 12; they were 308.6 and 33. DVE has not 87% of PE's work but as much as PE (308.6 beside 306.5 us), and behind step 12 it is busy for 92 to 94% of the time, where 79 to 90% was the sign of being right. Each operation of the sum was there, and its undisturbed duration was right: 0.42 for the conversion's first (0.42 said), 0.69 for the others. But the prices came from rows with an operand in PSUM, or in MoE 2, where GpSimd was busy for 2 of 137 us [rows 2, 8], and the change moved exactly these, the conversion and half of the q's, into SBUF, where a GpSimd operation holds them up. The failing sentence is "48 x (0.69 + 0.69 + 0.42)": with GpSimd beside it, it was 48 x (0.87 + 0.82 + 0.52), and q 0.85 instead of 0.61: 27 us more. Shortening GpSimd's operations gave 13.6 of the missing 20 us back, doubling one kind cost 19. The Trainium skill (GPSIMD Engine Reference, 1. Specifications) states that GpSimd's access to SBUF is shared with VectorE and that contention arises with VectorE instructions that read two SBUF inputs or run in a two-port mode; the trace agrees, with 844 at 726 ns on SBUF and 558 with an operand in PSUM. The one-source operation 705 is among those held up too (375 to 1452 ns); no run shows whether it runs in such a mode. The prediction weighed another rule and not this one.

What the short GpSimd run leaves above the forecast, 539.0 against 532.6, is smaller, and here the step "in the first 12 steps DVE stays the bound and costs about 5 us" failed: waits of some 20 us (326.9 us from its first to its last hidden matmul, less 306.5) where 12 were said. They lie in steps 1 to 12: 66.7 us there in the run with all three, against some 53 of matmuls counted in the order, a loss of 14. DVE is 88 to 91% busy there from 50 us on; of the waits that PE's list has in it, 3.3 us, 2.1 are for the copy between transposes and values, which has one buffer. The rest of those 14 us has no name in the list and stays open; so does what it costs that the planner holds `lock` operations apart, since the short run keeps the planned order. A second buffer for that copy was not tried.

**MoE 2 and end: right enough.** +1.4 was said; MoE 2's first score matmul comes 6.1 us earlier than before and the end 6.5, so nothing was lost, and without the rechecks nothing is gained.

**The rivals.** The case 'banks or DVE stay' (540 to 554, at 0.26) covers 552.6, though the range ends at 549. Of its two names the second came true: the waits stayed, since DVE's own operations grew, which no rival had. 'Banks' was near the time by luck: the list names no bank that was held long, and 13.6 us of the loss go with GpSimd. Its premise, that banks are scarce, shows with 3.5 us in the conversion through PSUM. The clock, which was bounded at 5 us for the start alone, is worth, by the slope of the last run's six times, some 4 us in the whole span for the 0.987 of the changed kernel's profile against the full clock of before; this is an estimate from that slope.
